# Linear attention and an MLP on one core: loads cast and cut by chunk, decays moved into masks, groups of four chunks

## The chip, the cores and the metric

One core of a Trainium2 chip. The time is the device time of one execution in microseconds (us); for each kernel several executions, quoted as a median. "Span" is the time from the first to the last instruction of the one execution that was profiled; here it is 1.5 us (before) shorter than the timed run.

## The reference, cut to what matters

Linear attention with a decay per head, over 4 batches, 8 heads, 768 positions and 64 dimensions, then an MLP of 512 to 2048 to 512 with exact gelu over the 3072 tokens.

```python
for b in range(nb):
    intra = (qb @ kb^T) * Dmask          # Dmask[i, j] = lam ** (i - j) for i >= j, else 0
    out   = intra @ vb + (qb * lam ** (i + 1)) @ kv_state
    kv_state = lam ** block * kv_state + (kb * lam ** (block - 1 - j))^T @ vb
x = out, heads side by side              # [3072, 512]
y = gelu(x @ w_in) @ w_out
```

The reference's `block` is 64. Both kernels work in chunks of 128 positions: 6 chunks a batch, 24 in all. "Attention of a chunk" is: transposes of q and k, scores, state product, mask, outputs. The MLP takes groups of chunks.

## The kernel before

GpSimd scales q by lam^i and v by lam^-i as they land in float32, SyncE loads whole batches ahead, and also stores the results. Group 0 has six chunks, whose attention (the "early" chunks) runs before any MLP; later attention is placed between the MLP matmuls of the group before it.

```python
groups = [6, 4, 4, 4, 4, 2]
...
def hats(n, early=False):
    ...
    nc.gpsimd.tensor_mul(c.q_hat, qkv[c.b, "q"][:, c.sb, :, :], lam_pos_b)     # L147
    nc.gpsimd.tensor_mul(c.v_hat, qkv[c.b, "v"][:, c.sb, :, :], lam_neg_b)     # L148
...
def load_batch(b):
    alloc_batch(b)
    for so in range(NB):
        for name in "qkv":
            load(nc.sync, b, name, so)                                         # L65
...
                    nc.scalar.copy(o_sb, om[io])                               # L234
                    nc.sync.dma_start(out[r:r + C, :], o_sb)                   # L235
```

## Time and profile before

| | us |
|---|---|
| median (3 runs: 253.48 to 254.13) | 253.85 |
| span | 252.3 |
| first MLP matmul (group 0, six chunks) | 37.8 |
| first matmul of group 1 | 99.1 |
| one steady period: 4 chunks of MLP, 4 of attention | 34.5 |

### The profile page before, as it was taken

The page shows a single profiled execution, that of the slowest core. Times are in us where ns is not written, and L with a number is a line of the kernel's source. Part 1 is how long each engine was busy: PE and PEld are TensorE (multiplying, and loading weights), DVE is VectorE, ACT ScalarE, POOL GpSimd, SP SyncE. Part 2 cuts the span into 40 slices and gives each one's busy share as a digit, 9 for nine tenths or more (in the row PEclk, how much of TensorE's full clock was granted, in tenths as well). Part 3 has the DMA queues.
Part 4 walks back from the last instruction along what each step waited for, and adds up shares of the span by engine and source line. Part 5 has one row for each costly group of instructions (what it writes and reads, how often), then busy time and mean ns, then how long its engine had stood idle before and what let it go on. Part 6 is the DMA issues. An engine that isn't in the chain of part 4 may idle for free.

```text
span 252.3 us, 3796 instructions
## 1 busy us (share of the span) xinstructions
PE 218.2 (86%) x1561; PEld 117.5 (47%) x1584; DVE 83.8 (33%) x136; ACT 83.5 (33%) x151; POOL 77.3 (31%) x81
## 2 busy tenths in 40 slices
PE   0156588999999339999999999999999999999994
PEld 0144454555555114445444554454555444444763
DVE  0449490014434202532543444334434413221000
ACT  3103037766100011463104551025521056410741
POOL 5959901110045400280031552900135414000000
PEclk9999999999999957999999999999999999999999
DMA  6999999999999980069993001120001210012102
GB/s 124 218 215 220 197 196 196 196 215 229 200 229 217 211 266 14 31 134 231 219 216 121 3 0 41 44 83 0 3 0 52 76 42 0 3 42 83 44 0 83
DMA packets 82864, 29.60 MB, mean 117 GB/s; under 512 B 75552, under 2 KB 79904, under 8 KB 82848
## 3 DMA queue, kind: packets, MB, share of 16 engines
q1 hardware_dynamic: 72384, 23.60, 44.6%
q0 software_dynamic: 4224, 4.19, 9.8%
q10 hardware_dynamic: 6240, 1.57, 3.6%
q8 instruction: 12, 0.20, 0.3%
q14 instruction: 4, 0.03, 0.1%
HBM read 27.27 MB, written 6.29 MB: 133 GB/s over the span
## 4 chain that ended last, share of the span: by engine, by line
PE 61%; SPq 34%; issue 2%; DMA 2%; ACT 1%; ACTq 0%
SPq L65 33%; PE o_ps L229 26%; PE h_ps L217 25%; PE o_ps L196 2%; PE sc_ps L165 2%; DMA out_dram<-o_sb 2%; PE kv_ps L173 1%; PE o_ps L244 1%; PE o_ps L192 1%; PE t_ps L156 1%; PE t_ps L154 1%; ACT o_sb L234 0%; SPq L71 0%; ACT o_sb L248 0%; ACT g_t L219 0%
## 5 line engine op out<-in xcount | busy, mean ns | idle before, releaser
L229 PE MATMUL o_ps<-w_out_t,g_t 128*128 128x512 bf16 x353 | 85.1, 387 | 8.7 <-ACT o_sb L234 7.8
L217 PE MATMUL h_ps<-x_t,w_in_t 128*128 128x512 bf16 (+2 forms) x440 | 89.7, 348 | 1.7 <-ACT g_t L219 1.0
L219 ACT ACTIVATE g_t<-h_ps 128x512 bf16<-128x512 f32 (+2 forms) x112 | 59.9, 536 | 38.9 <-PE h_ps L217 38.5
L217 PEld LDWEIGHTS <-w_in_t 128*128 128x128 bf16 x448 | 42.1, 97 | 38.9 <-issue 4.6
L229 PEld LDWEIGHTS <-g_t 128*128 128x128 bf16 x368 | 34.7, 99 | 46.5 <-issue 10.5
L185 POOL TENSOR_TENSOR state<-tmp,lam_blk 128x512 bf16<-128x512 f32 x12 | 16.1, 1345 | 110.1 <-DVE tmp L184 110.1
L234 ACT COPY o_sb<-o_ps 128x512 f32<-128x512 f32 x23 | 13.5, 586 | 94.1 <-PE o_ps L229 71.3
L177 DVE TENSOR_TENSOR sc_m<-sc_ps,cmask 128x512 bf16<-128x512 f32 x48 | 30.9, 684 | 41.1 <-PE sc_ps L165 41.0
L158 DVE COPY qkT<-t_ps 128x1024 bf16<-128x1024 bf16 x24 | 16.6, 691 | 63.3 <-PE t_ps L156 63.3
L148 POOL TENSOR_TENSOR v_hat<-v_t,lam_neg 128x512 bf16<-128x512 f32 x24 | 25.5, 1061 | 16.9 <-PE h_ps L217 15.3
L147 POOL TENSOR_TENSOR q_hat<-q_t,lam_pos 128x512 bf16<-128x512 f32 x24 | 25.1, 1046 | 7.3 <-DMA q_t<-in_q_dram 7.2
L154 PE MATMUL t_ps<-ident,q_hat 128*128 128x128 bf16 x96 | 10.6, 241 | 18.4 <-POOL q_hat L147 18.4
L202 DVE CAST x_t<-o_ps 128x512 bf16<-128x512 f32 x18 | 12.4, 691 | 33.7 <-PE o_ps L196 33.2
L154 PEld LDWEIGHTS <-q_hat 128*128 128x128 bf16 x96 | 7.6, 106 | 23.6 <-POOL q_hat L147 19.1
L156 PE MATMUL t_ps<-ident,k_bf 128*128 128x128 bf16 x96 | 10.7, 242 | 1.3 <-ACT k_bf L144 1.3
L196 PE MATMUL o_ps<-sc_m,v_hat 128*64 128x128 bf16 x192 | 11.4, 246 | 0.4 <-DVE sc_m L177 0.4
L200 ACT CAST x_t<-o_ps 128x512 bf16<-128x512 f32 x6 | 3.5, 585 | 22.6 <-PE o_ps L196 22.6
L165 PE MATMUL sc_ps<-qkT 64*128 64x128 bf16 x192 | 10.8, 240 | 0.1
L184 DVE TENSOR_TENSOR tmp<-kv_ps,state 128x512 f32<-128x512 f32 x16 | 10.9, 679 | 0.0
L165 PEld LDWEIGHTS <-qkT 64*128 64x128 bf16 x192 | 6.1, 103 | 8.7 <-issue 8.3
L196 PEld LDWEIGHTS <-v_hat 128*64 128x64 bf16 x192 | 7.0, 121 | 4.4 <-issue 2.8
L173 PE MATMUL kv_ps<-v_hat,k_bf 128*128 128x128 bf16 x80 | 9.0, 243 | 0.0
(31 smaller groups left out, 71.4 us busy)
## 6 DMA issues: line engine op xcount, KB each, us to landing
q_t<-in_q_dram SPq DMA_DIRECT2D x24, 256.0 KB, 5.2
v_t<-in_v_dram SPq DMA_DIRECT2D x24, 256.0 KB, 5.1
out_dram<-o_sb SPq DMA_DIRECT2D x23, 256.0 KB, 2.0
k_t<-in_k_dram SPq DMA_DIRECT2D x18, 256.0 KB, 5.1
w_in_t<-in_moe_w_in_dram POOLq DMA_DIRECT2D x4, 512.0 KB, 12.9
w_out_t<-in_moe_w_out_dram POOLq DMA_DIRECT2D x4, 512.0 KB, 23.4
k_t<-in_k_dram ACTq DMA_DIRECT2D x6, 256.0 KB, 6.9
out_dram<-o_sb SPq DMA_DIRECT2D x2, 128.0 KB, 1.7
```

Source lines behind the costliest of these rows:

```text
L65: eng.dma_start(qkv[b, name][:, so, :, :], dram[name][b, :, so * C:(so + 1) * C, :].rearrange("h si d -> si h d"))
L147: nc.gpsimd.tensor_mul(c.q_hat, qkv[c.b, "q"][:, c.sb, :, :], lam_pos_b)
L148: nc.gpsimd.tensor_mul(c.v_hat, qkv[c.b, "v"][:, c.sb, :, :], lam_neg_b)
L154: nc.tensor.transpose(t_ps[:, 0, hp * C:(hp + 1) * C], c.q_hat[:, 2 * hp:2 * hp + 2, :], ident)
L158: nc.vector.tensor_copy(c.qkT, t_ps)
L165: nc.tensor.matmul(sc_ps[hi][:, hp, :], c.qkT[hi * D:(hi + 1) * D, 1, hp * C:(hp + 1) * C], c.qkT[hi * D:(hi + 1) * D, 0, hp * C:(hp + 1) ...
L177: nc.vector.tensor_mul(c.sc_m[:, hi, :, :], sc_ps[hi], cmask_b)
L185: (nc.vector if c.early else nc.gpsimd).tensor_mul(new, tmp, lam_blk)
L196: nc.tensor.matmul(o_ps[hi * D:(hi + 1) * D, hp, :], c.v_hat[:, h, :], c.sc_m[:, hi, hp, :], start=(c.sb == 0 and hp == 0), stop=True, ski ...
L217: nc.tensor.matmul(h_ps, w_in_t[:, ki, kf * 128:(kf + 1) * 128], x_t[:, ki, sub * N:(sub + 1) * N], start=(ki == 0), stop=(ki == NK1 - 1))
L219: nc.scalar.activation(g_t[:, kf, sub * N:(sub + 1) * N], h_ps, ACT.Gelu)
L229: nc.tensor.matmul(om[io], g_t[:, kf, io * C:(io + 1) * C], w_out_t[:, kf, :], start=(kf == 0), stop=(kf == NK2 - 1))
```

## The change

Its intent: start the MLP earlier and keep loads out of its way. Loads go through GpSimd's queue, which casts them to bfloat16, chunk by chunk, four chunks ahead; the decays of q and of the scores move into evacuations that VectorE makes anyway (`lam_q`, `dmask`, whose powers come from squaring), only k still needs a multiplication (`k_dec`); the states are 64 by 64 a head instead of block-diagonal 128 by 128; all groups have four chunks; in group 0 two outputs take the slices of w_out side by side as they land.

```diff
-    groups = [6, 4, 4, 4, 4, 2]
+    M = 4
...
+    def load(n, name):
+        raw[n, name] = qkv_pool.tile([128, H, D], BF16, tag=name, name=f"{name}_t")
+        nc.gpsimd.dma_start(raw[n, name], chunk_of(name, n))
...
-        nc.gpsimd.tensor_mul(c.q_hat, qkv[c.b, "q"][:, c.sb, :, :], lam_pos_b)
-        nc.gpsimd.tensor_mul(c.v_hat, qkv[c.b, "v"][:, c.sb, :, :], lam_neg_b)
+            eng.tensor_mul(c.k_dec, c.k, lam_k[:, :, None].to_broadcast((128, H, D)))
...
+        nc.vector.tensor_mul(c.qT, t_ps[:, 1], lam_q)
...
-            nc.vector.tensor_mul(c.sc_m[:, hi, :, :], sc_ps[hi], cmask_b)
+            nc.vector.tensor_mul(c.sc_m[:, :, hi, :], sc_ps[hi], dmask_r[:, :, hi, :])
...
-                nc.vector.tensor_add(tmp, kv_ps, states[c.n])
-                (nc.vector if c.early else nc.gpsimd).tensor_mul(new, tmp, lam_blk)
+                nc.vector.tensor_add(new, kv_ps, states[c.n][1])
+            if c.sb < NB - 2:
+                (nc.vector if c.early else nc.gpsimd).tensor_mul(old, new, lam_c_b)
...
+        if g == 0:
+            blocks += [(mm2(io, part), 4 * 512) for pair in range(0, M, 2) for part in range(parts)
+                       for io in (pair, pair + 1)]
...
-            first = 0.35 if g == 0 else 0.0
+            first, end = (0.77, 1.0) if g == 0 else (0.0, 0.97)
...
                     if kind == 0:
-                        live[n] = hats(n)
+                        prefetch(n + 4)
+                        live[n] = begin(n)
+                        decay_k(live[n], nc.gpsimd)
```

## The prediction

> **What bounds the kernel now.** I read the table of engines by stage first, because shares on the page average over stages with different limits. I cut it where TensorE's kind of work changes.
>
> ```profile
> core 0: us, PE busy (x) PEld busy (x) DVE busy (x) ACT busy (x) POOL busy (x), PEclk, DMA share, GB/s
> 0.00:37.80 37.80, 17.73 (x184) 12.39 (x184) 20.90 (x32) 7.62 (x12) 25.64 (x34) 1.00 1.16 195
> 37.80:62.50 24.70, 23.71 (x161) 13.39 (x158) 3.60 (x6) 16.93 (x33) 3.13 (x3) 1.00 1.20 209
> 62.50:84.00 21.50, 21.18 (x160) 11.03 (x163) 8.47 (x14) 2.27 (x5) 6.75 (x6) 1.00 1.18 213
> 84.00:92.40 8.40, 0.59 (x4) 0.19 (x3) 1.30 (x3) 0.62 (x2) 3.26 (x3) 0.71 0.97 252
> ...
> 133.40:167.90 34.50, 34.14 (x249) 17.44 (x253) 13.81 (x23) 11.89 (x20) 14.46 (x14) 1.00 0.09 35
> ...
> 233.40:252.30 18.90, 15.15 (x112) 10.74 (x111) 0.00 (x0) 7.91 (x20) 0.00 (x0) 0.98 0.12 42
> ```
>
> These are two kernels in one. Up to 92 us the DMA engines are full (share about 1, some 200 GB/s): for 37.8 us TensorE is under half busy, then it works for 46 us, then it stands for 8 us at a lowered clock. From 99 us on the DMA share falls away and TensorE is 99% busy; one period of 34.5 us is four chunks of the MLP with four chunks of attention between.
>
> The waits of TensorE, and one of ScalarE, say what holds the first part:
>
> ```profile
> PE t_ps L154 <- POOL q_hat L147: 18.4, 4, 10.3
> PE o_ps L229 <- ACT o_sb L234: 7.8, 1, 7.8
> ...
> ACT o_sb L234 <- DMA out_dram<-o_sb: 15.2, 1, 15.2
> ```
>
> At the start TensorE waits for GpSimd, which scales q as it lands. The 7.8 us is a chain: the second matmul waits for an evacuation, that for a buffer whose store has not landed, and the store sits in SyncE's queue behind the loads of batches needed much later. Three more lines give rates: the chain of waits (start, duration, what), the timeline, and GpSimd's issues of w_in.
>
> ```profile
> 134.84 2.59 PE h_ps L217 x12
> 60.21 1.14 SPq L65 DMA_DIRECT2D v_t<-in_v_dram  x1
> L120 POOL DMA_DIRECT2D w_in_t<-in_moe_w_in_dram x4: 757/765/964, 20.8 to 23.2; - x4
> DMA to landing us min/median/max: 9.1/12.9/16.8
> ```
>
> A 512-column matmul takes 2.59/12 = 0.216 us. One 256 KB load from a full queue takes 1.14 us. GpSimd spends about 0.75 us to issue one slice of weights.
>
> **What the Trainium skill says.** "DMA: Bandwidth & Descriptors", section "SWDGE vs HWDGE vs iDMA": a cast in a DMA is possible only from GpSimd, whose cores write the descriptors in software. The kernel before agrees so far that its casting weight loads are the ones on GpSimd, and they occupy it for 757 to 964 ns each. The same page, "Issuing engines are not separate DMA queues": all issuers share the same 16 engines, so moving loads to GpSimd adds no bandwidth; the trace agrees (about 200 GB/s whether one queue or two are loading). "TensorE: Matmul & The Clock Gate", section "Wait — 56ns, not 53.3ns?": a warm matmul costs N/2.4 + 2.5 ns, 215.8 ns for 512 columns; the 0.216 us above agrees, so the steady part has no slack in its MLP matmuls. "SBUF — State Buffer", section "SBUF: two separate sides", warns that VectorE's two-port modes lock GpSimd out while it writes descriptors. No line of this trace shows it; I count it as a risk only.
>
> **The change part by part.** The end is set by T1, the time at which group 1's first matmul starts, plus what follows it.
>
> After T1 (before: 99.1 us). Groups 1 to 4 carry four chunks of MLP and four of attention each, as the 34.5 us period does. MLP is 128 matmuls x 0.216 = 27.65 us, so a chunk of attention costs (34.5 - 27.65)/4 = 1.7 us of TensorE. The change splits the state and inter products into twice as many half-size ones (8 instead of 4 a chunk each), with half the columns or in pairs that use different quarters of the array, as the scores already do (8 in the time of 4 transposes). I put that at no change, plus or minus 0.1 us a chunk. Scaling q moves from GpSimd (1.05 us) into VectorE's evacuation (0.69 us today), v's scaling goes into the mask; VectorE and GpSimd are far from full there, so this is worth nothing in time. 4 x 34.5 = 138 us. The last group is 27.7 us. The tail after the last matmul's start was 252.3 - 248.7 = 3.6 us and stays. Sum 169.3 us. For comparison, before has 153.2 us after its T1, for 18 chunks of MLP; in the changed kernel 20 are left.
>
> T1 itself. Loads are the currency. Before T1 the changed kernel must have 24 loads (chunks 0 to 7) and the weights, where the one before moves 54 loads and the weights by about 88 us. Weights: the eight slices land from 20.8 + 9.1 = 29.9 us to about 53.6 us, 3.4 us apart while some three loads squeezed between; (23.7 - 3 x 1.14)/7 = 2.9 us each alone. For a cast load I choose 1.3 us as an estimate: same 1024 runs of 256 bytes read as today's 1.14 us, plus a little for software descriptors. Then: 2.5 us to the first packet, 2.5 us for k and q of chunk 0 (direct), ten casts 13 us, eight slices 23 us, 1.5 us to landing: the weights are there at 42.5 us.
> TensorE up to then: chunk 3 has landed at 19 us and passes transposes, scores, mask, outputs and evacuation in 4.5 us, so group 0 starts at about 24 us (37.8 before). Its 64 first matmuls take 14 us plus some 2 us at the lower clock, to 40 us; the first pair of outputs takes 6.9 us, walking through w_out slices as they land (3.5 us of need for each first-matmul slice against 2.9 us of supply, so nearly no wait). It ends at about 47 us. The second pair with attention of chunks 4 to 7 needs 6.9 + 4 x 1.7 = 13.7 us, so TensorE alone would reach T1 at 61 us.
> But it waits for loads. GpSimd works in order, and each of its DMAs takes one of eight completion semaphores, so it waits for the one eight before. In the built order k_dec of chunk 7 stands behind the prefetch of chunk 11, whose last DMA waits for the 16th cast after the weights (k of chunk 9). So chunk 7's state product, and with TensorE's order everything behind it, waits for 16 casts: 16 x 1.3 = 20.8 us after 42.5, plus 2 us for stores of group 0 in between, 2 us for the issue and the multiply on GpSimd (1.05 us for its like today), 2 us for state product, outputs and evacuation. T1 = 69.3 us.
>
> Span: 69.3 + 169.3 = 238.6 us. Timed runs before are 1.5 us above the span (253.85 against 252.3), hence 240 us.
>
> What is hidden: the powers by squaring (some 40 tiny VectorE instructions instead of three 1.65 us powers on GpSimd and a 2.2 us copy) lie beside the first loads; so do the activation table load moved forward and the mask. The freed store queue removes the 7.8 us wait, which is part of the fall of T1, not an extra.
>
> **The rivals.** First, slow casts: 128-byte writes and software descriptors may cost more than 1.3 us a load. T1 carries 26 of them, so each 0.1 us costs 2.6 us; at 1.9 us the span is 254 and nothing is won. For it speaks that the trace has no small-run load on this queue; against it that the weights, also cast there, landed at a good pace. Second, GpSimd as the bound: if issue time goes with the runs, 1024 take 1.5 us against 0.75 for 512; after the weights 17 issues and some 3 us of multiplies make 28.5 us instead of 23, T1 about 75 and the time 246. Third, TensorE as the bound: if casts are cheap because they write half the bytes, T1 falls to 61 and the time to 232. Fourth, the split products cost more weight loads than I think: 0.15 us a chunk over 16 chunks is 2.4 us. In the steady part GpSimd needs three issues and two multiplies a chunk, 4 to 6.5 us of 8.6, so it should not bind there.
>
> **Range and chances.** The steady part is known within 3 us; T1 is 61 to 80. I take 240 us, 231 to 252 for 8 in 10. To be within 2% of before it must be above 248.8, that is T1 above 78: casts at 1.65 us, or GpSimd binding with worse. Faster 0.84, within 2% 0.12, slower 0.04.
>
> **What would show it.** By stage: group 0's first matmul at 22 to 27 us; its 14 us nearly without wait; then a stage of 20 to 25 us before group 1 with TensorE half idle, waiting for loads of k and q and for k_dec on GpSimd; group 1 at 65 to 75 us; then periods of 34 to 35 us. The wait of the evacuation for stores must be gone. I am wrong if cast loads take over 1.6 us from one landing to the next, if TensorE still waits for loads after T1, or if the period leaves 33.5 to 36 us.

## More of the kernel before

The views stand in the prediction. One row that its cut leaves out belongs to them: the last batch still loads between 99 and 133 us, without holding TensorE (stretch and length in us, busy time of PE, PEld, DVE, ACT and POOL, then clock, DMA share, GB/s).

```profile
99.10:133.40 34.30, 33.93 (x245) 17.14 (x249) 14.05 (x23) 11.89 (x20) 10.51 (x10) 1.00 0.81 166
```

## The result, and the profile after

The changed kernel takes 241.7 us (median of 4 runs, 241.0 to 243.05) against 253.81, a ratio of 0.953 (95% interval 0.948 to 0.958). Ratios here are the mean time of one kernel's runs over that of the other's of the same rounds, so not quite the ratio of the medians. Executions over 1.5% slower than the fastest of the same kernel are left out of the means. The prediction said 240, and its middle step, group 1 at 69.3 us, was met almost to the digit: 69.6 us. The question is whether it was met for the reason given.

The engines by stage in the changed kernel, cut at the same places (columns as before):

```profile
0.00:25.80 25.80, 13.02 (x152) 9.29 (x153) 20.64 (x64) 11.21 (x28) 21.13 (x29) 1.00 1.65 157
25.80:41.60 15.80, 15.48 (x63) 6.71 (x65) 0.00 (x0) 8.96 (x15) 7.33 (x9) 1.00 1.67 185
41.60:48.50 6.90, 6.90 (x34) 3.13 (x33) 0.00 (x0) 1.18 (x2) 6.51 (x8) 1.00 2.51 154
48.50:69.60 21.10, 16.45 (x183) 9.37 (x185) 12.81 (x23) 1.75 (x3) 11.44 (x14) 0.86 1.18 100
69.60:105.20 35.60, 35.06 (x278) 17.28 (x281) 13.01 (x23) 11.51 (x20) 16.07 (x19) 0.98 0.91 83
105.20:140.20 35.00, 34.47 (x278) 17.16 (x282) 13.34 (x24) 11.94 (x21) 17.80 (x21) 1.00 0.73 72
...
209.50:240.60 31.10, 27.71 (x143) 13.98 (x143) 0.00 (x0) 12.64 (x22) 0.00 (x0) 1.00 0.12 43
```

The MLP starts 12 us earlier, at 25.8 us. Its first matmuls and the first pair of outputs run nearly without a gap to 48.5 us. (The first matmuls, up to 29.8 us, took 0.43 us each, twice the 0.216 of later ones. The clock column says 1.00 there only because the trace has no clock record before 29.8 us.) Then comes the weak stage: 21.1 us with TensorE busy for 16.45 and a mean clock of 0.86. From 69.6 us on it is the steady kernel again. (GB/s count what is written; a cast load writes half of what it reads, so this column is not to be compared with the kernel before.)

What TensorE waited for in the changed kernel (in total, times, longest):

```profile
PE sc_ps L198 <- DVE qT L191: 7.6, 8, 3.4
PE t_ps L184 <- DVE pw L124: 5.9, 1, 5.9
PE kv_ps L205 <- POOL k_dec L178: 2.2, 1, 2.2
PE o_ps L262 <- issue: 0.9, 6, 0.2
```

The wait of 7.8 us for an evacuation is gone, as predicted. But no line names a load. TensorE waits for VectorE (qT) and once for GpSimd (k_dec); the 5.9 us are the start of the kernel, until the first chunk of k is there.

Where the span went, worked out from these tables: 24 chunks of MLP at 6.91 us (32 matmuls of 0.216) are 165.9 us in both kernels.

| us | before | after |
|---|---|---|
| until the first MLP matmul | 37.8 | 25.8 |
| MLP | 165.9 | 165.9 |
| attention after that: 18 x 1.71, 20 x 1.78 | 30.8 | 35.6 |
| tail after the last matmul's start | 3.6 | 3.6 |
| the rest: waits and lowered clock | 14.2 | 9.7 |
| span | 252.3 | 240.6 |

1.71 is (34.5 - 27.65)/4; 1.78 is the same from the mean of the three periods that lie between 105.2 and 209.5 us, 34.8 us. So the 11.7 us are 12.0 from the earlier start and 4.5 from waits, less 4.8 for two more chunks of attention outside the start and each being a little dearer. Most of the last row of "after" lies between 41.6 and 69.6 us: the work there is the second matmul of four chunks (64 x 0.216 = 13.8 us) and four chunks of attention (7.1 us), 20.9 us done in 28.0, so 7.1 us are lost. TensorE's waits in it are 2.2 us for qT, in four pieces, and 2.2 us for k_dec; most of the rest is a lowered clock from 63.9 us on (see e1).

The landings, read from the semaphores in the trace, show how far the supply was from the prediction: the last slice of w_out landed at 37.2 us (predicted 42.5), after it one cast load landed every 0.90 us (predicted 1.3), v of chunk 7 at 48.4 and k of chunk 9, for which the prediction let group 1 wait, at 51.4 us (predicted 63.3). The issues of the cast loads on GpSimd:

```profile
L66 POOL DMA_DIRECT2D v_t<-in_v_dram x24: 873/883/1054, 1.4 to 164.7; - x24
...
DMA to landing us min/median/max: 3.3/4.9/18.0
```

The chain of waits of the changed kernel is a trap here. These are its pieces before group 1 (start, duration, what):

```profile
19.35 17.87 DMA w_out_t<-in_moe_w_out_dram
37.50 0.88 POOL q_t L66
...
51.45 1.07 POOL k_dec L178
52.51 8.52 issue
61.07 0.61 POOL old L219
...
64.31 1.07 POOL k_dec L178
65.85 1.82 PE o_ps L262 x4
```

Read fast, it says: weights, then loads, then GpSimd, so supply. But between 52.5 and 61.07 us stands "issue", which means that the profile saw nothing to wait for. The timeline of the changed kernel tells what GpSimd waited for:

```profile
59.27 0.32 PE L205 MATMUL kv_ps<-v_t,k_dec 128*64 128x64 bf16 x8
60.58 0.41 DVE L214 CAST state<-kv_ps 128x256 bf16<-128x256 f32 x1
61.07 0.61 POOL L219 TENSOR_TENSOR old<-state,cpw 128x256 f32<-128x256 bf16 x1 [8.56 <-DVE state L214]
61.62 0.92 POOL L66 DMA_DIRECT2D k_t<-in_k_dram  x1
62.54 0.89 POOL L66 DMA_DIRECT2D q_t<-in_q_dram  x1
63.42 0.88 POOL L66 DMA_DIRECT2D v_t<-in_v_dram  x1
64.31 1.06 POOL L178 TENSOR_TENSOR k_dec<-k_t,lam_k 128x512 bf16<-128x512 bf16 x1
65.43 0.42 PE L205 MATMUL kv_ps<-v_t,k_dec 128*64 128x64 bf16 x8 [2.22 <-POOL k_dec L178]
```

GpSimd sat idle for 8.56 us, though everything that chunks 4 to 7 need had landed by 48.4 us and the load that its next issues depend on by 51.4. It waited for TensorE itself: `old`, the decayed state of chunk 6, needs that chunk's state product. Only then could it issue three prefetches that nobody needs yet, and only then make `k_dec` of chunk 7, for which TensorE waited 2.2 us. So two theories stand against each other. Supply (the prediction's): group 1 waits until enough casts have landed. Order: loads are there; TensorE's own order in this stage, packed too tightly for VectorE's evacuations and for GpSimd's queue, sets the start of group 1.

### The profile page after: what moved, and what is told of

Its sections match the earlier page's. It is cut to its first block, busy times and chain, and to the rows that moved or that the text cites. A ratio compares the mean times of both kernels' runs of the same rounds, so it can differ in the third digit from the quotient of the medians.

```text
span 240.6 us, 4008 instructions
## 1 busy us (share of the span) xinstructions
PE 217.7 (90%) x1652; PEld 110.5 (46%) x1680; DVE 85.8 (36%) x180; ACT 82.7 (34%) x149; POOL 95.1 (40%) x114
## 4 chain that ended last, share of the span: by engine, by line
PE 71%; POOL 12%; DMA 10%; issue 6%; ACT 0%; POOLq 0%
PE h_ps L250 29%; PE o_ps L262 28%; DMA w_out_t<-in_moe_w_out_dram 7%; POOL v_t L66 3%; PE t_ps L184 3%; DMA k_t<-in_k_dram 3%; POOL q_t L66 3%; PE o_ps L232 3%; PE o_ps L228 2%; PE sc_ps L198 2%; POOL k_t L66 2%; POOL k_dec L178 2%; PE kv_ps L205 2%; PE o_ps L277 1%; POOL w_in_t L93 1%
## 5 line engine op out<-in xcount | busy, mean ns | idle before, releaser
L250 PE MATMUL h_ps<-x_t,w_in_t 128*128 128x512 bf16 x371 | 88.8, 386 | 1.7 <-ACT x_t L236 0.7
L252 ACT ACTIVATE g_t<-h_ps 128x512 bf16<-128x512 f32 x96 | 57.3, 597 | 45.1 <-PE h_ps L250 44.4
L250 PEld LDWEIGHTS <-w_in_t 128*128 128x128 bf16 x384 | 36.5, 99 | 43.3 <-issue 4.1
L210 DVE TENSOR_TENSOR sc_m<-sc_ps,dmask 128x512 bf16<-128x512 f32 x48 | 30.9, 686 | 31.4 <-PE sc_ps L198 31.3
L238 DVE CAST x_t<-o_ps 128x512 bf16<-128x512 f32 x20 | 13.8, 692 | 38.7 <-PE o_ps L232 38.5
L66 POOL DMA_DIRECT2D v_t<-in_v_dram x24 | 21.5, 897 | 3.3 <-DMA w_out_t<-in_moe_w_out_dram 1.7
L66 POOL DMA_DIRECT2D q_t<-in_q_dram x23 | 20.5, 892 | 4.9 <-DMA w_out_t<-in_moe_w_out_dram 3.7
L66 POOL DMA_DIRECT2D k_t<-in_k_dram x23 | 20.9, 909 | 3.9 <-DMA w_out_t<-in_moe_w_out_dram 1.7
L178 POOL TENSOR_TENSOR k_dec<-k_t,lam_k 128x512 bf16<-128x512 bf16 x18 | 20.1, 1118 | 0.9 <-DMA k_t<-in_k_dram 0.7
L191 DVE TENSOR_TENSOR qT<-t_ps,lam_q 128x512 bf16<-128x512 bf16 x24 | 16.3, 681 | 0.0
L232 PE MATMUL o_ps<-sc_m,v_t 128*64 128x128 bf16 x192 | 11.6, 243 | 0.2 <-DVE sc_m L210 0.2
L184 PE MATMUL t_ps<-ident,q_t 128*128 128x128 bf16 x96 | 10.5, 239 | 0.7 <-ACT q_t L165 0.7
```

Source lines behind the costliest of these rows:

```text
L66: nc.gpsimd.dma_start(raw[n, name], chunk_of(name, n))
L178: eng.tensor_mul(c.k_dec, c.k, lam_k[:, :, None].to_broadcast((128, H, D)))
L184: nc.tensor.transpose(t_ps[:, i, hp, :], src[:, 2 * hp:2 * hp + 2, :], ident)
L191: nc.vector.tensor_mul(c.qT, t_ps[:, 1], lam_q)
L210: nc.vector.tensor_mul(c.sc_m[:, :, hi, :], sc_ps[hi], dmask_r[:, :, hi, :])
L232: nc.tensor.matmul(o_ps[hi * D:(hi + 1) * D, hp, :], c.v[:, 2 * hp + hi, :], c.sc_m[:, hp, hi, :], start=(c.sb == 0 and hp == 0), stop=Tru ...
```

## The experiments

Each edit is of the changed kernel, except e4 and e7, which are of the kernel before. All gave correct results. Runs of different calls were on different chips, so ratios to the kernel before (run beside each) are what is compared; the changed kernel's is 0.953.

**e1: k_dec ahead of the prefetch.**

```diff
+    prefetch(2 * M - 1)                    # after the w_out slices
...
-                        prefetch(n + 4)
                         live[n] = begin(n)
                         decay_k(live[n], nc.gpsimd)
+                        prefetch(n + 4)
```

> The changed kernel with k_dec of each chunk put ahead of the prefetch in GpSimd's order (loads of chunks 4 to 7 are issued before any of it, the rest after). Theory order: group 1 starts late because TensorE waits 2.2 us for k_dec of chunk 7, which stands on GpSimd behind the old state of chunk 6 and three issues of 0.9 us; here only the old state is ahead of it, so it is ready at about 62.8 us instead of 65.4, TensorE's wait is gone, and group 1 starts 2 to 4 us earlier (the rest if the lowered clock goes too): 238 to 240 us against 241.7. Theory supply (that of the prediction): group 1 waits for casts to land; their order on the DMA queue is the same, so the start stays within 0.5 us and the time at 241 to 242.

237.4 us (236.97 to 237.59), ratio 0.936. Group 1 started at 65.1 us. GpSimd and TensorE at chunk 7 in e1's timeline:

```profile
60.25 0.61 POOL L219 TENSOR_TENSOR old<-state,cpw 128x256 f32<-128x256 bf16 x1 [8.31 <-DVE state L214]
...
60.83 1.03 POOL L178 TENSOR_TENSOR k_dec<-k_t,lam_k 128x512 bf16<-128x512 bf16 x1
...
62.31 0.32 PE L205 MATMUL kv_ps<-v_t,k_dec 128*64 128x64 bf16 x8
```

The wait is gone, with the same loads in the same order. Group 1 starts 4.5 us earlier, which is more than the wait of 2.2. Of this 0.8 us is not the edit's: this execution is ahead by as much from the first MLP matmul on (25.0 us against 25.8). Another 1.4 us is the clock: from chunk 7's state product to group 1 pass 2.75 us here and 4.16 in the changed kernel. The table by stage around it, in the changed kernel and then in e1 (last three columns: clock, DMA share, GB/s):

```profile
60.40:63.90 3.50, 1.65 (x25) 1.09 (x24) 2.88 (x7) 0.58 (x1) 2.83 (x4) 1.00 0.46 93
63.90:70.70 6.80, 5.05 (x38) 2.80 (x40) 2.62 (x6) 0.58 (x1) 5.69 (x7) 0.50 1.23 111
```

```profile
60.40:65.00 4.60, 3.28 (x52) 2.08 (x50) 3.83 (x8) 0.59 (x1) 4.59 (x6) 1.00 0.68 92
```

After 3.5 us in which TensorE was busy for less than half, the changed kernel ran 6.8 us at half clock; e1 did not drop at all there.

**e2: six spare loads.**

```diff
         load_w_out(s)
+    for i in range(6):
+        spare = consts.tile([128, H, D], BF16, name=f"spare{i}")
+        nc.gpsimd.dma_start(spare, chunk_of("kqv"[i % 3], NCH - 1 - i // 3))
```

> The changed kernel with six more cast loads, into tiles that nothing reads, between w_out and chunk 4. At 0.9 us from landing to landing they push the landings of chunks 4 to 9 back by 5.4 us: v of chunk 7 from 48.4 to about 53.8 us, k of chunk 9 from 51.4 to 56.8. Theory supply: group 1 starts 5.4 us later, 247 us. Theory order: chunk 4 has landed at 40 us and is needed at 49.3, chunk 7 at 48.4 and needed at 61.0, so all still come in time: no change within 1 us, 241 to 242.5.

242.56 us (241.98 to 244.47), ratio 0.958, an interval (0.952 to 0.963) that overlaps the changed kernel's. The loads did move: v of chunk 7 landed at 53.7 us, k of chunk 9 at 58.1 (a little later than expected). Group 1 started at 69.3 us. Chunk 7 in e2's timeline:

```profile
61.83 0.61 POOL L219 TENSOR_TENSOR old<-state,cpw 128x256 f32<-128x256 bf16 x1 [3.41 <-DVE state L214]
...
65.07 1.06 POOL L178 TENSOR_TENSOR k_dec<-k_t,lam_k 128x512 bf16<-128x512 bf16 x1
66.19 0.32 PE L205 MATMUL kv_ps<-v_t,k_dec 128*64 128x64 bf16 x8 [2.23 <-POOL k_dec L178]
```

The state product moved by 0.8 us (65.43 to 66.19), where the loads moved by 5 to 7: the supply had more than 5 us to spare, which the theory that it sets the start doesn't allow. The small cost has a cause of its own: k_dec of chunk 4 now stands behind later landings, and TensorE waited 1.0 us for it (its waits for k_dec total 3.3 us instead of 2.2). That group 1 then started no later is partly chance: the half clock lasted 3.4 us in this execution, 6.8 in the changed kernel's.

**e3: w_out in turn.**

```diff
-        if g == 0:
+        if False:
             blocks += [(mm2(io, part), 4 * 512) for pair in range(0, M, 2) ...
```

> The changed kernel without the w_out slices side by side: group 0's outputs one after the other as in the other groups. The last slice of w_out has landed at 37.2 us and the second matmul starts at 41.6, so the walk by slices has nothing to wait for. Theory that the side-by-side order still counts (weights late, as predicted at 42.5 us): 3 us slower or more. Theory that it is idle now: within 1 us of 241.7.

241.09 us (239.78 to 241.53), ratio 0.950: no difference shown. The side-by-side order is idle, because in the changed kernel the last slice lands at 37.2 us and the first matmul that reads w_out starts at 41.6. It is a remedy for late weights, and they are no longer late.

**e4: the kernel before, its stores on ScalarE's queue.**

```diff
-                    nc.sync.dma_start(out[r:r + C, :], o_sb)
+                    nc.scalar.dma_start(out[r:r + C, :], o_sb)
```

(and the same for the two half stores at the end)

> The kernel before, with only its stores issued by ScalarE's queue, so that none stands behind loads in SyncE's. Theory that the blocked store is worth its wait plus the cold clock after it: TensorE's 7.8 us wait goes, and of the 10.2 us at half clock most of the loss of 5: 241 to 246 us instead of 253.8. Rival, that the wait moves elsewhere (GpSimd's q_hat waits for loads of the same crowded DMA engines): 249 us or more.

247.86 us (247.39 to 248.0), ratio 0.977 (0.973 to 0.981). It fell between the two expectations. The wait shrank but did not vanish, as TensorE's waits in e4 show:

```profile
PE t_ps L154 <- POOL q_hat L147: 18.5, 4, 10.3
PE o_ps L229 <- ACT o_sb L234: 2.2, 1, 2.2
```

Group 1 started at 91.7 us instead of 99.1. So of the 12 us that the change gained, nearly half can be had by moving the stores to another queue than the loads.

**e7: the kernel before, with e4's edit and groups of four.**

```diff
-    groups = [6, 4, 4, 4, 4, 2]
+    groups = [4, 4, 4, 4, 4, 4]
```

> The kernel before with two small edits: stores on ScalarE's queue (e4: 247.9 us) and groups of four chunks. None of the casts in loads, the mask decays or the compact states. Chunk 3's x was ready at 35.1 us in the kernel before, so the MLP starts near 34 us instead of 37.7, and the last group of two with its 256-column matmuls (1.7 us dearer) is gone, but two more chunks of attention come after the start (3.4 us). Theory that the early start of the changed kernel (25 us) comes from its decays and loads and not from the group size: 246 to 249. Rival, that the group size brings most of it: 243 or less.

246.15 us (median of 4, 244.25 to 248.23), ratio 0.967. It started the MLP at 30.3 us, not near 34 as expected, so 7.4 of the 12.0 us of earlier start can be had from the smaller first group alone (e4 starts at 37.7). But it then lost part of that. TensorE's waits in e7:

```profile
PE t_ps L154 <- POOL q_hat L147: 15.7, 4, 10.9
PE o_ps L229 <- DMA w_out_t<-in_moe_w_out_dram: 2.4, 1, 2.4
PE h_ps L217 <- DMA w_in_t<-in_moe_w_in_dram: 2.2, 1, 2.2
```

Here the weights are late, behind float32 loads of whole batches, and here the side-by-side order would have had something to do. Group 1 started at 71.6 us, only 2 us after the changed kernel's. With two small edits the old design comes within 1.5% of the new one (0.967 against 0.953).

**e5: attention of group 0 over both pairs.**

```diff
-            first, end = (0.77, 1.0) if g == 0 else (0.0, 0.97)
+            first, end = (0.6, 1.0) if g == 0 else (0.0, 0.97)
```

> The changed kernel with the attention of chunks 4 to 7 spread from 0.60 of group 0 instead of from 0.77: one chunk every 2.7 us of MLP work instead of every 1.6. Theory order (TensorE waits for VectorE and GpSimd because four chunks stand too close at the end of group 0): each chunk's waits for qT (0.3 to 1.2 us) and the one for k_dec of chunk 7 shrink, group 1 starts at 63 to 65 us instead of 69.6, time 235 to 238. Theory supply: chunks 4 to 7 are needed earlier than now, so TensorE waits for the same landings and group 1 does not start earlier: 241 to 243.

236.97 us (236.41 to 237.5), ratio 0.934; group 1 at 64.2 us. Its first transposes of chunk 4 stand at 43.3 us instead of 49.4. Asking for the chunks 6 us earlier made it faster: the loads were lying there.

**e6: e5 and e1 together.** (both edits above)

> The edits of e5 and e1 together. If both take away the same waits (theory order), the two gains do not add: group 1 at 62 to 64 us, 234.5 to 237. If they were independent the gains would add to some 8 to 9 us, 233 or less.

235.27 us (234.93 to 236.09), ratio 0.927; group 1 at 62.7 us. e1 alone took 1.7 points off the ratio and e5 alone 1.9, together 2.6: they remove partly the same waits, and the half-clock stage, of which the profile of either alone is already free.

**e8: transposes one chunk ahead, in the early chunks.**

```diff
-    for s in range(M + 1):
-        if s < M:  begin(s); transposes(s); decay_k(s)
-        if s >= 1: outputs(s - 1)
-        if s < M:  scores(s)
+    for s in range(-1, M + 1):
+        if s + 1 < M:  begin(s + 1); transposes(s + 1); decay_k(s + 1)
+        if 0 <= s < M: scores(s)
+        if s >= 1:     outputs(s - 1)
```

(shortened; the calls keep their arguments)

> The changed kernel with the transposes and the two evacuations of the next chunk put ahead of the scores of this one, in the four early chunks only. Theory that VectorE sets the start of the MLP (in the early chunks it works 2.8 us of every 3.35 and idles the 0.67 us between qT and the scores): the idle time is filled three times, the MLP starts at 23 us instead of 25, and the time falls by 1.5 to 2.5 us to about 239.5. Rival, that the landing of chunk 3 (v at 15.3 us) or of w_in (21.5 us) sets it: no change.

239.82 us (239.04 to 240.83), ratio 0.945 (0.941 to 0.949). The MLP started at 24.1 us; the changed kernel's start was 25.8 in its profile and 25.0 in those of e1, e2, e3 and e5, which do not touch it. So it gained about half of the 2 us expected at the start; what else the ratio gained was not traced. Neither the landing of chunk 3 (15.3 us) nor that of the first slice of w_in (17.3 us) holds the start; the order of work on TensorE and VectorE does at least in part. What holds the rest was not tried.

**e9: state products whole.**

```diff
-                    nc.tensor.matmul(kv_ps[hi * D:(hi + 1) * D, hp, :], c.k_dec[:, h, :], c.v[:, h, :],
+                nc.tensor.matmul(kv_ps[:, hp, :], c.k_dec[:, 2 * hp:2 * hp + 2, :], c.v[:, 2 * hp:2 * hp + 2, :],
...
+                    nc.vector.tensor_add(new[p], kv_ps[p, :, p], states[c.n][1][p])   # for both halves p
```

> The changed kernel with the state product as in the kernel before: four products of 128 by 128 a chunk instead of eight of 64 by 64, the evacuation takes the two diagonal halves in two VectorE instructions; states stay compact. Theory that the split products cost TensorE weight loads: a steady period of four chunks is 34.6 to 35.0 us in the changed kernel and 34.3 to 34.5 before, so this undoes about half of that, 0.1 to 0.3 us a period, 241 us. Rival, that the split costs nothing: periods unchanged, 241.5 to 242.5 (two more VectorE instructions lie beside TensorE's work).

242.47 us (241.41 to 243.64), ratio 0.953. The second and third periods took 34.9 and 34.65 us, against 35.0 and 34.7: twice as many state products cost TensorE nothing that shows here. Why the period of the changed kernel is 0.3 us longer than the one before stays open; the products of q with the state, which are split in the same way, were not tried alone.

**e10: all of placement.** e1, e8, and in group 0:

```diff
-            first, end = (0.77, 1.0) if g == 0 else (0.0, 0.97)
+            first, end = (0.53, 1.0) if g == 0 else (0.0, 0.97)
...
-                fs = (-0.3, 0.0, 0.4, 1.0) if g == 0 else (-0.3, 0.0, 0.35, 0.75)
+                fs = (-0.3, 0.0, 0.5, 1.0) if g == 0 else (-0.3, 0.0, 0.35, 0.75)
```

> The changed kernel with the edits of e1 and e8 and attention spread from 0.53 of group 0, scores half a chunk after the transposes. Theory order: the MLP starts at 24 us, TensorE's waits in group 0's second half all but vanish, its work there is 13.8 us of MLP and 7.1 of attention, so group 1 starts at 60 to 61.5 us and the time is 231.5 to 234. If loads begin to bind (v of chunk 5 lands at 43, chunk 6 at 45.4, chunk 7 at 48.4 us, all still ahead of their need at 44.5, 49 and 53.5), group 1 stays at 62.7 and the time at 235.

233.78 us (median of 5, 233.44 to 234.48), ratio 0.919 (0.917 to 0.922): it beats both kernels. The table by stage in e10:

```profile
24.10:38.90 14.80, 14.53 (x55) 6.09 (x57) 0.00 (x0) 7.76 (x13) 5.93 (x7) 1.00 1.47 187
38.90:62.00 23.10, 22.78 (x221) 11.85 (x223) 12.52 (x23) 4.13 (x7) 17.74 (x22) 1.00 1.98 136
```

The stage before group 1 is full, at full clock. Group 1 started at 62.3 us, a little over the 60 to 61.5 expected, in part because the first 64 matmuls of the MLP took 16.5 us in this execution (14.9 to 16.3 in the profiles of the changed kernel and its other variants; 13.8 would be full clock throughout). The same loads as in the changed kernel now serve a start 7 us earlier.

## Why the prediction was right or wrong

The time was right, 240 against 241.7, and so was the sum for what follows group 1's start (169.3 us predicted, 171.0 measured: the first period is 1.1 us longer, half of it through the clock that stays lowered until 70.7 us, the others 0.1 to 0.5 us). Point by point:

- **What binds at the start, and the wait for stores.** Right: the wait is gone, the MLP starts at 25.8 us (24 predicted). But chunk 3 landed at 15.3 us, not 19, and the reason given (its landing plus 4.5 us) did not hold; the order of work in the early chunks does in part (e8 shifts the start by 0.9 us without touching a load).
- **The weights at 42.5 us.** Wrong term: 37.2 us. The cast loads took 0.9 us each, not 1.3, and the slices 2.6 us from landing to landing, not 2.9.
- **"But it waits for loads": the step that failed.** The prediction let chunk 7's k_dec, and with it group 1, wait for the 16th cast after the weights, 69.3 us. The 16th landed at 51.4. With this landing and its own 6 us for the rest, the prediction's sum would give 57.4 us, less than its bound for TensorE. e2 pushed the landings back by 5 to 7 us and chunk 7's state product moved by 0.8; e1 moved it from 65.4 to 62.3 us (0.8 of that from its earlier start) with the same loads in the same order. What the runs showed in its place: k_dec of chunk 7 does stand behind the prefetch of chunk 11 in GpSimd's order, as the prediction had read from the built order, but ahead of both stands `old` of chunk 6, and that waits for TensorE. The queue was held by a dependency on the engine that then waited for the queue. Nor was TensorE "half idle" before group 1: it was busy for 16.45 of 21.1 us.
- **"TensorE alone would reach T1 at 61 us."** This bound was right (e10 reached 62.3). The prediction took it for the third rival, at 232 us, and gave that rival too little: cheap casts were the fact. But cheap casts alone did not give 232, because the schedule placed four chunks of attention in the last 23% of group 0, where each waits for VectorE. Two errors cancelled: casts too dear (69.3 - 61 = 8.3 us), and the waits on VectorE and GpSimd with the lowered clock after them left out (69.6 - 61 = 8.6 us). That T1 was met to 0.3 us is luck.
- **The second rival, GpSimd's issue at 1.5 us a load.** Wrong: 0.88 us for 1024 runs, against 0.78 for 512. GpSimd did hold TensorE once, by its order and not by its issue time.
- **The fourth, split products.** Not shown: e9 undid half of them without effect.
- **"From 99 us on the DMA share falls away".** A misreading: between 99.1 and 133.4 us it was still 0.81. Nothing rested on it, since TensorE did not wait there.

And what of the change brought the gain? e4 and e7 in turn take the kernel before from a ratio of 1 to 0.977 and 0.967; the casts, masks and compact states with their new order make the step to 0.953; they were not tried one by one. Their larger gift, chunks that land 10 us and more before they are used (k of chunk 4 at 38.1 us, used at 49.4), lay idle until e5 and e10 placed the work to use it, e10 at 0.919.

## What to carry to other kernels

A number that comes out right confirms nothing about its steps: push the supposed bound back on purpose (six spare loads) and see whether the end moves. On an engine that works in order, put what another engine waits for ahead of prefetches, and look for a queue that is held by a result of the very engine that will wait for it. When a change makes the supply earlier, move the demand too; and never let a store queue behind loads that are needed later.

## What the Trainium skill lacked or had wrong

- "DMA: Bandwidth & Descriptors", section "Bandwidth", has no rate for casting loads of short runs from GpSimd's queue. Here 256 KB read as 1024 runs of 256 bytes, and written as 1024 of 128, landed every 0.90 us when queued, faster than the same read by a direct queue (1.14 us).
- The same page, section "Anatomy of one DMA", calls descriptor generation "small, variable". Here an issue held GpSimd for 0.87 to 1.05 us with 1024 runs and 0.75 to 0.83 us with 512: not small, though nearer to the first-byte time of about 1 us that the page gives elsewhere. What it lacks is that this time lies in one order with GpSimd's arithmetic: three issues (2.7 us) stood ahead of one k_dec.
- "TensorE: Matmul & The Clock Gate", section "What's actually happening", gives the half clock after an idle window of about 3.4 us, and not how idle it must be (nor does the page where it names frequent short idles as a cause). Here it came after 3.5 us in which TensorE was busy for 1.65 us, with no wait over 2.2 us, and stayed for 6.8 us.
- "SBUF — State Buffer", section "SBUF: two separate sides", on VectorE and GpSimd locking each other out, agrees for arithmetic: k_dec took 2.04 us beside the making of dmask (1.21 us on VectorE) and 1.04 to 1.09 alone. Its warning for descriptors was not seen: issues stayed at 0.88 to 0.95 us (the first 1.05) while VectorE was busy 9.2 us of 10 (5 to 15 us); in which of its modes it ran there, the trace doesn't tell.
- No page says that a chain of waits followed back through "issue" may have lost its cause: here 8.52 us of it were GpSimd waiting for TensorE.
